# Scores on two row tiles, DMA transposes in chosen chunks, and a planner with priority tables in a fused attention and feed-forward kernel

## Chip, cores and metric

One core of a Trainium2 chip. The metric is the device time of one execution in microseconds. An execution has a state: slow ones (over 1.5% above the fastest of the same kernel) are set aside. The profiler also records the clock that was granted to TensorE; its mean is called "the clock" below (1.0 is full). A ratio of two kernels is the mean of one's fast runs over the mean of the other's fast runs in the same rounds, so it is not quite the ratio of the medians that are quoted.

## The reference

```python
# B, H, S, D = 4, 8, 768, 48;  d_model = 384, d_ff = 2048
f = 1 / (1 + exp(-f_logit))
for t in range(S):                                  # gated linear attention
    state = f[:, :, t, :, None] * state + einsum('bhd,bhe->bhde', k[:, :, t], v[:, :, t])
    y[:, :, t] = einsum('bhd,bhde->bhe', q[:, :, t], state)
x = y.transpose(0, 2, 1, 3).reshape(B * S, H * D)   # 3072 tokens x 384
h = x @ w_in
out = (h * cos(h)) @ w_out
```

## The kernel before

The sequence is cut into 24 chunks of 128 tokens. For a chunk, ScalarE turns f into running decays (an exponential, a logarithm, then two exponentials `b` and `bi` of sums that TensorE makes). q is multiplied by `b`, k by `bi`; both are transposed; TensorE makes scores, masked by VectorE, then the output y, which is transposed into x. Feed-forward units of 128 or 256 tokens follow: product with w_in, cosine on ScalarE, product on VectorE, product with w_out. Every operation is an object with candidate engines, a duration and a priority. A planner in Python, run at build time, lists them in one static order; each engine then runs its part strictly in that order.

```python
def chunk_load(b, c, prio):
    for pool, src in ((fS, f_logit), (vS, v), (kS, k), (qS, q)):
        eng, dma = {"SP": 650.0}, nc.sync
        if prio < 1 and pool in (kS, qS):            # chunk 0 only
            eng, dma = {"ACT": 600.0}, nc.scalar
        elif prio < 1 and pool is vS:
            eng, dma = {"POOL": 850.0}, nc.gpsimd
        ...

# scores: 128 rows of contraction; k of even and odd heads in two copies,
# zero where the other head's rows are
for g in range(2):
    def pe(e, g=g, pa=pa):
        for i in range(4):
            h = 4 * g + i
            nc.tensor.matmul(o[:, i, :], lhsT=kz[g].ap[:, i, :], rhs=qdt.ap[:, h // 2, :], ...)
...
# order: the earliest possible start wins, then the priority
key = (pick[1], o.prio, o.seq)
...                                                  # (cut)
pr = LEAD + RATE * n0 + 0.5 * span * j * G / KF      # first product:  2 + chunk number
pr = LEAD + LAG + RATE * n0 + 0.5 * span + 0.5 * i   # second product: 7 + chunk number
GATES = [1, 2, 3, 4]      # w_out transfers wait for k of these chunks; w_in for chunk 0
```

Of the kernel before, what the change touches and what calls it, by code (L numbers as in the profile page):

```python
# [9 lines left out]
F32 = mybir.dt.float32  # L10
# [86 lines left out]
class Plan:  # L97


    SEM = 70.0  # L100
    RING = 3500.0
# [4 lines left out]
    def op(self, eng, fn, reads=(), writes=(), prio=0.0, table=None, lat=0.0, grp=None, dma=0.0):  # L106
# [6 lines left out]
        for v in writes:  # L113
            w = getattr(v, "whole", v)
            if w.pool is not None:
                o.alloc.append(w)
            if v.writers:

                o.deps.add(v.writers[-1])
        for v in list(reads) + list(writes):  # L120
            v = getattr(v, "whole", v)
            if v.pool is not None and v not in o.vals:
                o.vals.append(v)
                v.uses += 1
# [11 lines left out]
    def run(self):  # L136
        engs = ("PE", "ACT", "DVE", "POOL", "SP")
        free = dict.fromkeys(engs, 0.0)
# [13 lines left out]
        while len(order) < n:  # L152
            best = None
            for o in ready:
                at = max([d.end + (0.0 if e0 == d.eng == "PE" else self.SEM)
                          for d in o.deps for e0 in (next(iter(o.eng)),)], default=0.0)
                ok = True
                for v in o.alloc:
                    if v.slot is not None:
                        continue  # L160
                    b = v.pool.best()
                    if b is None:
                        ok = False
                        break
                    at = max(at, b[0] + self.SEM)
                if not ok:
                    continue
# [12 lines left out]
                key = (pick[1], o.prio, o.seq)  # L180
                if best is None or key < best[0]:
                    best = (key, pick[1], o, pick[2], pick[3])
            assert best is not None, "no op can be placed: " + str(
                [(o.seq, o.eng, o.prio, lock, o.grp, [v.pool.name for v in o.alloc]) for o in ready])
            _, s, o, e, cost = best
# [14 lines left out]
            if o.dma:  # L200
                q = int(e == "POOL")
                t = max(ring[q], s + cost)
# [3 lines left out]
                rate = (0.94 if q else 0.25) if large else 0.6  # L206
# [5 lines left out]
                ring[1 - q] += both * (1.0 - (0.25 if q else 0.94)) if large else 0.4 * both  # L212
# [23 lines left out]
def kernel(  # L236
# [21 lines left out]
    GROUPS = [1] * 4 + [2] * 10  # L258
    FAST, LAG = 24, 5.0
    GATES = [1, 2, 3, 4]  # L260
    NPE, NPX, EVERY = 8, 24, 1
    LEAD, RATE = 2.0, 1.0
    UNITS = [128] * 4 + [256] * 10
# [6 lines left out]
    make_identity(nc, ident)  # L270
    umask = cpool.tile([128, 128], BF16, name="umask")
    make_upper_triangular(nc, umask, val=1.0, diag=True)
# [25 lines left out]
    qkS = slots("qk", 3, [128, 3 * NP * C], zero=700.0)  # L298
    qktS = slots("qkt", 4, [128, 3 * NP, C])
    amS = slots("am", 4, [128, 4, C])  # L300
    szS = slots("sz", 3, [128, NP, 2 * D])
    yS = slots("y", 3, [128, d_model])
    stS = slots("st", 2, [128, NP, 2 * D], F32)
# [13 lines left out]
    P = Plan()  # L317
    for pool, cost in zeroed:
# [10 lines left out]
    def load_weights(part, i, prio):  # L329
# [8 lines left out]
        gate(o, 0 if part == 0 else GATES[i])  # L338
# [5 lines left out]
    k_done, gated = {}, {}  # L344

    def gate(o, n):

        if n in k_done:
            o.deps.add(k_done[n])
        elif n >= 0:  # L350
            gated.setdefault(n, []).append(o)

    def chunk_load(b, c, prio):
        vals = []
        for pool, src in ((fS, f_logit), (vS, v), (kS, k), (qS, q)):
            t = Val(pool)
            ap = src[b, :, c * C:(c + 1) * C, :].rearrange("h p d -> p h d")
            eng, dma = {"SP": 650.0}, nc.sync
            if prio < 1 and pool in (kS, qS):
                eng, dma = {"ACT": 600.0}, nc.scalar  # L360
            elif prio < 1 and pool is vS:
                eng, dma = {"POOL": 850.0}, nc.gpsimd
            P.op(eng, lambda e, t=t, ap=ap, dma=dma: dma.dma_start(out=t.ap, in_=ap),  # L363
                 writes=[t], prio=prio, lat=2000.0, dma=980.0)
# [3 lines left out]
    def decay_group(chunks, g, prio):  # L368

        outs = []  # L370
        for (b, c, ld) in chunks:
# [8 lines left out]

            e1 = P.op({"ACT": 515.0}, act1, reads=[f], writes=[f], prio=prio, table="E", grp=g)
            P.op({"ACT": 515.0}, act2, reads=[f], writes=[sp], prio=prio, table="E", grp=g)
# [4 lines left out]
        for (b, c, ld, sp) in outs:  # L387
# [15 lines left out]
            P.op({"ACT": 400.0}, ex, reads=[pc], writes=[bt], prio=prio, table="E", grp=g)  # L403
            P.op({"ACT": 400.0}, lambda e, pc=pc, bi=bi, ex=ex: ex(e, pc, bi, 1.0, H * D),
# [4 lines left out]
    def attend(b, c, ld, bt, bi, prio):  # L409
        _, v32, kf, qf = ld  # L410
# [3 lines left out]
        qtd = qk.part(lambda a: a[:, 0:NP * C].rearrange("p (h d) -> p h d", d=64)[:, :, 0:D])  # L414
        ktd = [qk.part(lambda a, par=par: a[:, NP * C:].rearrange(
            "p (n r d) -> p n r d", r=4, d=64)[:, :, 3 * par, 0:D]) for par in range(2)]
        fast = tok < FAST * C
        E = lambda e: nc.vector if e == "DVE" else nc.gpsimd
        P.op({"POOL": 1000.0, "DVE": 560.0} if fast else {"POOL": 1000.0}, lambda e: E(e).tensor_mul(  # L419
            out=qtd.ap, in0=qf.ap,  # L420
            in1=bt.ap[:, 0:H * D].rearrange("p (h d) -> p h d", d=D)),
            reads=[qf, bt], writes=[qtd], prio=prio)
        for par in range(2):
            o = P.op({"POOL": 550.0, "DVE": 350.0} if fast and tok else {"POOL": 550.0}, lambda e, par=par: E(e).tensor_mul(  # L424
                out=ktd[par].ap, in0=kf.ap[:, par:H:2, :],
                in1=bi.ap.rearrange("p (h d) -> p h d", d=D)[:, par:H:2, :]),
                reads=[kf, bi], writes=[ktd[par]], prio=prio)
        vf = Val(vbS)
        P.op({"POOL": 510.0}, lambda e: nc.gpsimd.tensor_copy(out=vf.ap, in_=v32.ap),  # L429
             reads=[v32], writes=[vf], prio=prio)  # L430
        k_done[tok // C] = o
# [6 lines left out]
        kz = [qkt.part(lambda a, g=g: a[:, (g + 1) * NP:(g + 2) * NP, :]) for g in range(2)]  # L438
        if tok < NPE * C or tok // C % EVERY:
            for g in range(3):  # L440
                pqk = Val(miS)

                def tr(e, g=g, pqk=pqk):
                    o = pqk.ap.bitcast(BF16).rearrange("p (a n) -> p a n", n=C)
                    for i in range(NP):
# [3 lines left out]
                P.op({"PE": 4 * N128}, tr, reads=[qtd] if g == 0 else ktd, writes=[pqk],  # L449
                     prio=prio, lat=170.0)  # L450

                def evac(e, g=g, pqk=pqk):
                    o = pqk.ap.bitcast(BF16).rearrange("p (a n) -> p a n", n=C)
                    d, s = qkt.ap[:, g * NP:(g + 1) * NP, :], o[:, 0:NP, :]
                    if e == "ACT":
                        nc.scalar.copy(out=d, in_=s)
                    else:
                        nc.vector.tensor_copy(out=d, in_=s)
                P.op({"DVE": 425.0, "ACT": 500.0}, evac, reads=[pqk],
                     writes=[qdt if g == 0 else kz[g - 1]], prio=prio)  # L460
        else:
            P.op({"SP": 1400.0}, lambda e: nc.sync.dma_start_transpose(out=qkt.ap, in_=qk.ap),  # L462
                 reads=[qtd] + ktd, writes=[qdt] + kz, prio=prio, lat=2000.0, dma=2100.0)

        ams = []
        for g in range(2):
            pa, am = Val(paS), Val(amS)

            def pe(e, g=g, pa=pa):
                o = pa.ap.rearrange("p (a n) -> p a n", n=C)  # L470
                for i in range(4):
                    h = 4 * g + i
                    nc.tensor.matmul(o[:, i, :], lhsT=kz[g].ap[:, i, :],  # L473
                                     rhs=qdt.ap[:, h // 2, :], start=(i == 0), stop=(i == 3))
            P.op({"PE": 4 * N128}, pe, reads=[kz[g], qdt], writes=[pa], prio=prio, lat=170.0)

            def mask(e, pa=pa, am=am):
# [3 lines left out]
            P.op({"DVE": 670.0}, mask, reads=[pa], writes=[am], prio=prio)  # L481
            ams.append(am)
# [3 lines left out]
        if c < NCH - 1:  # L486
            ps, S_out = Val(miS), Val(szS)

            def pes(e):
                o = ps.ap[:, 0:H * D].rearrange("p (h d) -> p h d", d=D)  # L490
                for h in range(H):
                    nc.tensor.matmul(o[:, h, :], lhsT=qk.ap[:, (NP + h) * C:(NP + h + 1) * C],
                                     rhs=vf.ap[:, h, :],
                                     start=(h == 0), stop=(h == H - 1))
            P.op({"PE": 8 * 25.0}, pes, reads=ktd + [vf], writes=[ps], prio=prio, lat=170.0)
            psv = lambda: ps.ap[:, 0:H * D].rearrange("p (a n) -> p a n", n=2 * D)
            if S_in is None:
                src, srcap, cost = ps, psv, {"DVE": 550.0}
            else:
                st = Val(stS)  # L500
                P.op({"DVE": 530.0}, lambda e: nc.vector.tensor_add(  # L501
                    out=st.ap, in0=psv(), in1=S_in.ap),
                    reads=[ps, S_in], writes=[st], prio=prio)
                src, srcap, cost = st, (lambda: st.ap), {"POOL": 1000.0}
            P.op(cost, lambda e: E(e).tensor_mul(  # L505
                out=S_out.ap, in0=srcap(),
                in1=bt.ap[:, H * D:, None].broadcast_to([128, NP, 2 * D])),
                reads=[src, bt], writes=[S_out], prio=prio)
# [5 lines left out]
        def pey(e):  # L514
            o = py.ap[:, 0:H * D].rearrange("p (h d) -> p h d", d=D)
            for h in range(H):
                nc.tensor.matmul(o[:, h, :], lhsT=ams[h // 4].ap[:, h % 4, :], rhs=vf.ap[:, h, :],  # L517
# [11 lines left out]
        P.op({"ACT": 380.0, "DVE": 530.0}, copy(lambda: yt.ap, lambda: py.ap[:, 0:H * D]),  # L529
             reads=[py], writes=[yt], prio=prio)  # L530
        x = xT[tok // C]
        if tok < NPX * C:
# [8 lines left out]
            P.op({"ACT": 380.0, "DVE": 330.0}, copy(lambda: x.ap, pxv), reads=[px], writes=[x],  # L541
# [6 lines left out]
    def moe(t0, T):  # L548
# [6 lines left out]
        for j in range(KF // G):  # L555
# [10 lines left out]
            pr = LEAD + RATE * n0 + 0.5 * span * j * G / KF  # L566
# [91 lines left out]
```

## Time and profile before

| | before |
|---|---|
| median of 3 runs | 200.21 us (199.2 to 202.75, the last one slow) |
| profiled execution, its span | 198.71 us, 196.9 us |
| busy: TensorE, ScalarE, VectorE, GpSimd | 88%, 74%, 72%, 30% |

The span goes from the first to the last instruction of the trace; runs are some 2 us longer. The lines of the profile are in the prediction. "PE" is TensorE, "DVE" VectorE, "ACT" ScalarE, "POOL" GpSimd, "SP" SyncE, which issues most loads. A "q" behind an engine's name marks its instruction queue, for instance the time that issuing a load takes it. Busy time of TensorE contains the depth of its pipeline (a 384-column product is recorded as 326 ns, while in a burst one starts every 162.5), so this document counts **full-rate work**: how many matmuls started in a stretch, times the time one takes in a long burst. Stretch minus work is **lost time**.

### The profile page before, as it was taken

What the parts mean: (1) busy time and instruction counts of PE and PEld (TensorE: products, weight loads), DVE (VectorE), ACT (ScalarE), POOL (GpSimd) and SP (SyncE); (2) the same over time, 40 slices, a digit from 0 to 9 for tenths busy, and PEclk for the clock granted to TensorE, in tenths of its full rate; (3) what the DMA queues carried; (4) which work ended last, traced back from release to release, by engine and by line L of the source; (5) the groups of instructions that cost most, each with busy time, mean ns of one, the idle gap of its engine ahead of it and who ended that gap; (6) DMA issues with size and microseconds to landing.
All of it is one profiled execution on the core that took longest, in us unless ns stands there. A gap on an engine that the chain in (4) does not pass through costs nothing.

```text
span 196.9 us, 5063 instructions
## 1 busy us (share of the span) xinstructions
PE 173.7 (88%) x1968; PEld 135.7 (69%) x1968; DVE 141.3 (72%) x256; ACT 146.0 (74%) x263; POOL 58.2 (30%) x94
## 2 busy tenths in 40 slices
PE   0388987696899978999999999999999999999993
PEld 0167884485687766887876886877777788868661
DVE  5178865867897937956967978869999998928200
ACT  4457688597987975968968988989999996729210
POOL 7395104162412734205114214122332601000000
PEclk9999999999999999999999999999999999999999
DMA  7999998999899999999999999999999341020122
GB/s 139 217 179 194 188 196 173 184 202 183 163 217 190 222 171 248 234 191 223 165 226 192 212 229 192 226 221 194 221 206 260 91 97 45 0 80 3 40 80 82
DMA packets 131144, 33.36 MB, mean 169 GB/s; under 512 B 124416, under 2 KB 131072, under 8 KB 131120
## 3 DMA queue, kind: packets, MB, share of 16 engines
q1 hardware_dynamic: 125264, 29.30, 73.8%
q0 software_dynamic: 3776, 3.34, 10.7%
q10 hardware_dynamic: 2080, 0.39, 1.1%
q8 instruction: 15, 0.25, 0.5%
q14 instruction: 9, 0.07, 0.1%
HBM read 25.17 MB, written 4.72 MB: 152 GB/s over the span
## 4 chain that ended last, share of the span: by engine, by line
PE 42%; DMA 24%; DVE 11%; SPq 7%; POOL 5%; ACT 4%; issue 4%; DVEq 0%; POOLq 0%; ACTq 0%
PE ps L583 18%; PE ps L562 17%; DMA w_out_bf<-in_moe_w_out_dram 10%; DMA qkt<-qk 6%; SPq L363 5%; DMA q<-in_q_dram 4%; DMA v<-in_v_dram 4%; DVE gT L573 3%; PE ps L473 3%; DVE am L478 2%; DVE qk L419 2%; SPq L462 2%; POOL w_in_bf L336 2%; PE ps L517 1%; DVE y L527 1%
## 5 line engine op out<-in xcount | busy, mean ns | idle before, releaser
L583 PE MATMUL ps<-w_out_bf,gT 128*128 128x384 bf16 x384 | 71.2, 326 | 2.4 <-DMA w_out_bf<-in_moe_w_out_dram 2.2
L562 PE MATMUL ps<-xT,w_in_bf 128*128 128x256 bf16 (+1 forms) x672 | 69.3, 257 | 1.5 <-DVE xT L527 0.8
L562 PEld LDWEIGHTS <-w_in_bf 128*128 128x128 bf16 x672 | 57.3, 98 | 8.8 <-DVE xT L527 0.9
L573 DVE TENSOR_TENSOR gT<-ps,cosh 128x512 bf16<-128x512 f32 x96 | 60.1, 681 | 3.6 <-ACT cosh L569 3.5
L569 ACT ACTIVATE cosh<-ps 128x512 bf16<-128x512 f32 x96 | 53.7, 604 | 8.7 <-PE ps L562 6.0
L583 PEld LDWEIGHTS <-gT 128*128 128x128 bf16 x384 | 35.2, 97 | 21.1 <-issue 2.2
L478 DVE TENSOR_TENSOR am<-ps,umask 128x512 bf16<-128x512 f32 x48 | 31.0, 682 | 13.0 <-PE ps L473 12.9
L429 POOL CAST vb<-v 128x384 bf16<-128x384 f32 x24 | 12.7, 531 | 43.2 <-DMA v<-in_v_dram 28.2
L424 POOL TENSOR_TENSOR qk<-k,bi 128x192 bf16<-128x192 f32 x30 | 19.2, 650 | 20.0 <-ACT bi L401 10.2
L505 POOL TENSOR_TENSOR sz<-st,b 128x384 bf16<-128x384 f32 x16 | 13.6, 848 | 38.1 <-DVE st L501 29.1
L419 DVE TENSOR_TENSOR qk<-q,b 128x384 bf16<-128x384 f32 x20 | 13.4, 668 | 12.7 <-DMA q<-in_q_dram 7.5
L473 PE MATMUL ps<-qkt 128*128 128x128 bf16 x192 | 16.5, 225 | 2.5 <-DMA qkt<-qk 2.5
L592 ACT COPY ot<-ps 128x384 f32<-128x384 f32 x14 | 6.7, 478 | 15.2 <-PE ps L583 15.2
L625 ACT ACT_TABLE_LOAD x12 | 15.4, 1283 | 2.2 <-issue 2.0
L401 ACT ACTIVATE b<-ps 128x388 f32<-128x388 f32 x24 | 12.1, 503 | 6.2 <-PE ps L394 6.0
L569 ACT ACT_TABLE_LOAD x12 | 15.4, 1283 | 0.2
L376 ACT ACTIVATE f<-f 128x384 f32<-128x384 f32 x24 | 11.7, 518 | 4.4 <-DMA f<-in_f_logit_dram 4.3
L473 PEld LDWEIGHTS <-qkt 128*128 128x128 bf16 x192 | 12.3, 100 | 3.8 <-DMA qkt<-qk 2.8
L447 PE MATMUL ps<-ident,qk 128*128 128x128 bf16 x96 | 9.3, 242 | 5.2 <-DVE qk L419 3.2
L391 PE MATMUL ps<-sp,umask 128*128 128x384 bf16 x24 | 8.1, 346 | 5.6 <-ACT sp L379 5.2
L527 ACT CAST y<-ps 128x384 bf16<-128x384 f32 x16 | 7.7, 480 | 6.7 <-PE ps L520 3.8
L401 ACT ACTIVATE bi<-ps 128x384 f32<-128x384 f32 x24 | 12.0, 500 | 0.0
(37 smaller groups left out, 156.2 us busy)
## 6 DMA issues: line engine op xcount, KB each, us to landing
f<-in_f_logit_dram SPq DMA_DIRECT2D x24, 192.0 KB, 4.1
out_dram<-ot SPq DMA_DIRECT2D x24, 192.0 KB, 2.7
v<-in_v_dram SPq DMA_DIRECT2D x23, 192.0 KB, 4.0
k<-in_k_dram SPq DMA_DIRECT2D x23, 192.0 KB, 3.8
q<-in_q_dram SPq DMA_DIRECT2D x23, 192.0 KB, 4.3
w_in_bf<-in_moe_w_in_dram POOLq DMA_DIRECT2D x4, 384.0 KB, 9.7
w_out_bf<-in_moe_w_out_dram POOLq DMA_DIRECT2D x4, 384.0 KB, 8.3
qkt<-qk SPq DMA_TRANSPOSE x16, 4.0
```

Source lines behind the costliest of these rows:

```text
L401: nc.scalar.activation(out=o.ap, in_=pc.ap[:, 0:n], func=AF.Exp, scale=s)
L419: P.op({"POOL": 1000.0, "DVE": 560.0} if fast else {"POOL": 1000.0}, lambda e: E(e).tensor_mul(out=qtd.ap, in0=qf.ap, in1=bt.ap[:, 0:H * D ...
L424: o = P.op({"POOL": 550.0, "DVE": 350.0} if fast and tok else {"POOL": 550.0}, lambda e, par=par: E(e).tensor_mul(out=ktd[par].ap, in0=kf. ...
L429: P.op({"POOL": 510.0}, lambda e: nc.gpsimd.tensor_copy(out=vf.ap, in_=v32.ap), reads=[v32], writes=[vf], prio=prio)
L473: nc.tensor.matmul(o[:, i, :], lhsT=kz[g].ap[:, i, :], rhs=qdt.ap[:, h // 2, :], start=(i == 0), stop=(i == 3))
L478: nc.vector.tensor_mul(out=am.ap, in0=pa.ap.rearrange("p (a n) -> p a n", n=C), in1=umask[:, None, :].broadcast_to([128, 4, C]))
L505: P.op(cost, lambda e: E(e).tensor_mul(out=S_out.ap, in0=srcap(), in1=bt.ap[:, H * D:, None].broadcast_to([128, NP, 2 * D])), reads=[src, ...
L562: nc.tensor.matmul(ph.ap[:, g * T:(g + 1) * T], lhsT=w_in_bf[:, m, f0:f0 + 128], rhs=x[:, m, :], start=(g == 0 and m == 0), stop=(g == G - ...
L569: P.op({"ACT": 570.0}, lambda e, ph=ph, co=co: nc.scalar.activation(out=co.ap, in_=ph.ap, func=AF.Sin, bias=HALF_PI), reads=[ph], writes=[ ...
L573: P.op({"DVE": 650.0}, lambda e, ph=ph, co=co, gv=gv: nc.vector.tensor_mul(out=gv.ap, in0=ph.ap.rearrange("p (g t) -> p g t", t=T), in1=co ...
L583: nc.tensor.matmul(po.ap[:, 0:d_model], lhsT=gT.ap[:, j, i * 128:(i + 1) * 128], rhs=w_out_bf[:, j, :], start=(j == 0), stop=(j == KF - 1))
L625: nc.scalar.preload_act_table_set("natural_log_exp_and_others")
```

## The change

The intent: cheaper scores, less work for the DMA engines, and an order in which TensorE waits less. The planner's durations are also brought nearer to a trace. The diff, cut to its core:

```diff
-    GROUPS = [1] * 4 + [2] * 10
-    FAST, LAG = 24, 5.0
-    GATES = [1, 2, 3, 4]
-    NPE, NPX, EVERY = 8, 24, 1
-    LEAD, RATE = 2.0, 1.0
-    UNITS = [128] * 4 + [256] * 10
+    GROUPS = [1, 1, 1, 1, 1, 1, 2, 2, 2, 2, 1, 1, 3, 2, 3]
+    UNITS = [128, 128, 128, 128, 256, 256, 256, 256, 128, 128, 256, 256, 256, 256, 128, 128]
+    ATT = [-10.16, -8.17, ...]       # 24 numbers each: attention, decay groups,
+    DEC = [-0.66, -1.41, ...]        # first product, second product
+    MM1 = [6.38, -2.33, ...]
+    MM2 = [8.02, 8.08, ...]
+    GATES = [1, 0, 0, 0, 2, 3, 2, 2]
+    QUEUES = ["SAAA", "ASSA", "SSSS", ...]           # f, k, q, v: S SyncE, A ScalarE
+    QK_DMA = [7, 10, 13, 14, 15, 17, 18, 19, 20, 21, 22, 23]
+    X_DMA = [11, 13, 15, 18, 19, 20, 22, 23]
+    FAST = 12
@@ the planner's choice
-                key = (pick[1], o.prio, o.seq)
+            # per engine: best priority among those that can start within WAIT of the first
+            for p in sorted(picks, key=lambda p: p[:2]):
+                if p[4] not in best and p[2] <= first[p[4]] + self.WAIT.get(p[4], 0.0):
+                    best[p[4]] = p
@@ loads
-            if prio < 1 and pool in (kS, qS): ... nc.scalar
-            elif prio < 1 and pool is vS: ... nc.gpsimd
+            way = QUEUES[min(b * NCH + c, len(QUEUES) - 1)][len(vals)]
@@ scores (q and k each in one block of four, two heads of 48 rows per 128)
+        def pe(e):
+            for p in range(NP):
+                for g in range(2):
+                    nc.tensor.matmul(pas[g].ap[:, p * C:(p + 1) * C],
+                                     lhsT=kdt.ap[64 * g:64 * g + D, p, :],
+                                     rhs=qdt.ap[64 * g:64 * g + D, p, :], ...)
```

(Cut: the state update in four products of two heads with its additions split by rows, the transposes, new durations.)

## The prediction

> **What bounds the kernel now.** I read four views, in this order: the page's head (busy time, slices, queues), the groups of instructions, the same busy times cut into three stages, and the chain of waits. First the head:
>
> ```profile
> span 196.9 us, 5063 instructions
> PE 173.7 (88%) x1968; PEld 135.7 (69%) x1968; DVE 141.3 (72%) x256; ACT 146.0 (74%) x263; POOL 58.2 (30%) x94
> PE   0388987696899978999999999999999999999993
> DMA  7999998999899999999999999999999341020122
> q1 hardware_dynamic: 125264, 29.30, 73.8%
> q0 software_dynamic: 3776, 3.34, 10.7%
> q10 hardware_dynamic: 2080, 0.39, 1.1%
> ```
>
> Two resources are full. TensorE is ragged over the first third and full after it; the DMA engines are full until slice 31 (155 us) and then nearly idle. VectorE and ScalarE stay near three quarters. The stages say where TensorE loses:
>
> ```profile
> core 0: us, PE busy (x) PEld busy (x) DVE busy (x) ACT busy (x) POOL busy (x), PEclk, DMA share, GB/s
> 0.00:50.00 50.00, 34.66 (x485) 28.32 (x486) 33.54 (x67) 33.03 (x57) 21.40 (x39) 1.00 1.10 186
> 50.00:155.00 105.00, 101.00 (x1151) 79.16 (x1150) 85.55 (x155) 90.78 (x168) 34.65 (x53) 1.00 1.02 206
> 155.00:197.00 42.00, 38.04 (x337) 28.18 (x334) 22.24 (x37) 22.19 (x41) 2.16 (x3) 1.00 0.19 58
> ```
>
> Busy time counts the pipeline's depth with every short burst, so I work with full-rate time instead, read off long bursts in the chain of waits:
>
> ```profile
> 27.51 2.68 PE ps L562 x48
> 38.25 1.46 PE ps L583 x8
> 74.61 0.62 PE ps L473 x8
> 109.95 0.65 PE ps L583 x4
> 110.60 3.93 PE ps L562 x36
> 114.53 0.45 PE ps L473 x8
> 116.93 0.20 PE ps L517 x8
> 117.13 0.17 PE ps L520 x4
> ```
>
> So one matmul takes, at full rate, 3.93/36 = 109 ns at 256 columns, about 57 ns at 128 columns (2.68/48 and 0.45/8), 0.65/4 = 162.5 ns at 384, 25 ns at 48 and 43 ns at 96. With the counts of the groups: second product 384 x 162.5 = 62.4; first product 480 x 109 + 192 x 57 = 63.3; scores 192 x 56 = 10.8; q/k transposes 96 x 56 = 5.4; scores times v 192 x 25 = 4.8; state update 160 x 25 = 4.0; state read 80 x 43 = 3.4; x transposes 72 x 56 = 4.0; decay sums 6.3. Sum **164.5 us** of work in a span of 196.9, so TensorE loses 32.4. Doing the same sum with the counts of the first 50 us gives about 29 of work: 21 are lost there. The last matmul ends at 193.6: 3.3 for the last copy and store. The remaining 8 are spread over 50 to 193 us. The lost time of the first 50 us is fill (the first chunk's chain) and weights that come late:
>
> ```profile
> 13.09 13.55 DMA w_out_bf<-in_moe_w_out_dram
> 31.95 6.25 DMA w_out_bf<-in_moe_w_out_dram
> ```
>
> **DMA is a second bound of almost the same size.** Queue q10 carried two input loads in 1.1% of 196.9 = 2.17 us, so 1.08 us of all 16 engines each. A store costs about 0.54 (share 0.19 over the last 7 us, some two and a half stores). q1 took 145.3 us: 93 loads 100.4, 24 stores 13.0, which leaves 31.9 for 16 transposes, 2.0 each. A late chunk costs the DMA 4 x 1.08 + 2.0 + 0.54 = 6.9 us, and TensorE 164.5/24 = 6.85. The loads feed it just fast enough, never ahead.
>
> **What the Trainium skill says.** TensorEngine Tiling (Array Packing), sections Theoretical Speedup and Key Properties: a contraction of at most 64 rows may run up to twice as fast as two row tiles working in parallel, and changing the tiling mode drains TensorE. The trace of before has only 128*128 forms, so it shows neither. TensorE: Matmul & The Clock Gate, section Back-to-back issue gap: columns/2.4 + 2.5 ns, 56 at 128 columns; bursts here agree (56), not with its 81 for sustained pairs. ScalarE: Activation LUTs, section What ACT_TABLE_LOAD costs: 1283 ns plus a drain of about 1380. The trace has 24 loads of 1283, while idle time before the twelve at L569 sums to 0.2 us, so I count no drain. DMA: Bandwidth & Descriptors, section Specifications: line rate needs 512 B or more. The loads have rows of 48 floats, 192 B; 1.08 us for 196,608 B is 182 GB/s, and the change leaves those rows alone.
>
> **The change part by part.** Counts come from the changed kernel's built instruction order.
> - Scores: still 192 matmuls, now 48 rows of contraction on two 64-row tiles, alternating between tiles and two banks. Fully parallel they cost 5.4 us, not parallel 10.8. The new planner figure is 330 ns a chunk, 7.9 us; I take that: **-2.9**, before any drain.
> - x transposes on TensorE: 72 become 48: -1.3. State update: 160 x 25 becomes 80 x 43: -0.6. Four more units of 128 tokens: 96 x 109 becomes 192 x 57: +0.4. q/k transposes stay 96: chunks come in two groups rather than three, but 12 chunks instead of 8. TensorE: 164.5 - 4.4 = **160.1**.
> - DMA: 12 transposes of two thirds the size, 12 x 1.33 = 16.0, plus 8 of x at a quarter, 8 x 0.5 = 4.0, in place of 31.9: **-12**. The DMA per chunk falls to about 5.7 on average, 1 us below TensorE's 6.7, so that loads can run ahead; most transposes sit in chunks 13 and later.
> - ScalarE: table loads 24 to 18, -7.7; xT copies 12 to 5, y copies 16 to 19, q/k copies 5 to 3: some -3.5. Busy 146 to about 135. VectorE: q and k products fall from 20 + 18 halves (23.2 us) to 19 whole (about 12); the split state additions (64 rows, 192 elements) add 2 to 3: 141 to about 132. GpSimd takes 29 whole products of about 1.0 us in place of 4 + 30 halves (23.2): about 68. All three have room; this mainly shortens waits of TensorE, so I do not add it.
> - Weights: all eight transfers were gated after k of chunks 0 to 4 (GpSimd issues 9.5 to 42.1 us). Now w_in follows v of chunks 0 and 1, and w_out v of chunks 2 and 3. The first chunk itself gains little: ScalarE issues five loads before its first table load, the fifth waiting for an earlier one to land, which may delay its first exponential from 4.1 to about 6; in return k no longer queues on GpSimd.
> - Order: tables of priorities and a planner with other durations decide which chunk and unit goes first. This removes no work; it decides how much of the 32 lost microseconds stays.
>
> Sum. Lost in the first 50 us: 21 less 4.5, since the 3.5 us weight waits beside w_out and the holes that followed between 30 and 50 (some 6 lost there) should mostly close: 16.5. Lost from 50 to the last matmul: 8 less 3, as the loads run ahead: 5. Tail 3.3. So 160.1 + 24.8 = a span of 184.9. The runs exceed the span: the profiled execution by 1.8 us (198.71 against 196.9), the lowest run by 2.3. I add 1.6, leaning to the fast side since the tables look searched for: **186.5 us**.
>
> **The rivals.**
> 1. Drain takes the tiling's gain. Each chunk switches mode in and out, 48 switches; an isolated 128-column matmul lasts 219 ns against 56 at full rate, so a full drain may be some 160 ns (an estimate from these). That is up to 7.7 us, more than the 2.9 saved; then 190 to 192. For it: short runs of scores between other work. Against: the planner's 330 ns looks like a measurement, and two drains might overlap with weight loads.
> 2. DMA still sets the pace early. Weights (21 us of q0) and the first six chunks (26 us) fill the DMA for 47 us whatever the order; earlier weights push chunk loads back, and TensorE loses again what it gained. Then the 21 stays near 20 and the time is 190. The full DMA row of slices 1 to 9 speaks for it; against it, TensorE needs only two or three chunks once the weights are in.
> 3. The order works much better than I allow: lost time in the first 50 us down to 13, in the middle to 2, and full parallel scores: a span near 176, 178 us. For it: 24-entry tables come from a search. Against: a planner's static order is only as good as its durations, and in-order queues stop at each wrong guess.
> 4. GpSimd's longer chain (q and k product, 2 us, then cast, from chunk 12 on) starves a late chunk. At about 3.6 us a chunk against 6.7 it can only hurt in latency.
>
> **Range and chances.** Centre 186.5; rivals 1 and 2 bring it to 190 to 192, both together to 195; rival 3 to 178. Range 180 to 192. Two per cent faster means under 196.2, which needs only a third of the sum: faster 0.95, within 2% 0.04, slower 0.01.
>
> **What would show it.** Right: score groups in a 64*128 form with about 41 ns between starts; full-rate work of TensorE near 160; hardware queue q1 about 12 us shorter; 18 table loads; DMA row falling off before 150 us; the first w_out waits gone and 5 us less lost in the first 50 us. Wrong: gaps of over 100 ns around each score group (rival 1); loads or v casts still waited for between 20 and 50 us (rival 2); ScalarE or VectorE over 85% busy in the middle, which would make one of them the bound; or a new long hole where one engine waits in order for a late piece.

## The result

The changed kernel is correct. Its median is **194.13 us** (193.2 to 194.2, 4 runs) against 199.81 for the kernel before (now 4 runs); the ratio is 0.971 (95% interval 0.967 to 0.975). The direction was right; the time lies outside the predicted range of 180 to 192, and the gain is 6 us in place of 14.

The head of the page of the changed kernel (busy times, the 40 slices, the queues):

```profile
span 192.4 us, 5056 instructions
PE 170.5 (89%) x1960; PEld 129.5 (67%) x1960; DVE 138.0 (72%) x259; ACT 137.4 (71%) x250; POOL 65.6 (34%) x105
PE   0056996879999999999999999999999999999992
PEclk9999997899999999999999999999999999999999
DMA  6999999998995999996399899799993383102022
q1 hardware_dynamic: 114096, 26.55, 68.9%
q10 hardware_dynamic: 5200, 0.98, 3.1%
```

Against the kernel before, TensorE starts later (the first slices read 0 0 5 6 in place of 0 3 8 8) and is at 9 from slice 10 on, without the dips that the kernel before has until slice 16. The row PEclk, all 9 before, has a 7 and an 8 in slices 7 and 8. The first two of the three stages that the prediction shows for the kernel before:

```profile
core 0: us, PE busy (x) PEld busy (x) DVE busy (x) ACT busy (x) POOL busy (x), PEclk, DMA share, GB/s
0.00:50.00 50.00, 32.70 (x416) 26.03 (x417) 33.15 (x66) 31.15 (x51) 17.95 (x35) 0.97 1.11 187
50.00:155.00 105.00, 104.00 (x1201) 78.69 (x1200) 83.98 (x159) 87.93 (x165) 42.77 (x64) 1.00 0.90 183
```

In the first 50 us only 416 matmuls began; before it was 485. In full-rate work, lost us of each stretch (each matmul counted once, in the stretch in which it starts; a tiled score counted at 41 ns):

| kernel | 0 to 25 | 25 to 50 | 50 to 150 | after the last matmul |
|---|---|---|---|---|
| before | 14.3 | 7.7 | 5.9 | 3.4 |
| changed | 17.9 | 6.7 | 3.6 | 3.6 |
| changed, two loads later (below) | 15.9 | 5.1 | 3.5 | 3.6 |
| changed, f first (below) | 14.6 | 5.9 | 3.5 | 3.6 |

So the middle is better than it was, and the start worse. TensorE's waits in the first 50 us say the same: it waits 9.4 us for its first input in place of 5.2, and no longer for weights, where before it waited 2.6. Why it is worse stands in the timeline of ScalarE and its queue; first the kernel before, then the changed kernel (columns: start, us, engine, line, what; in brackets the idle time ahead and what ended it):

```profile
0.73 0.48 ACTq L363 DMA_DIRECT2D k<-in_k_dram  x1
1.24 0.74 ACTq L363 DMA_DIRECT2D q<-in_q_dram  x1
2.02 1.28 ACT L625 ACT_TABLE_LOAD   x1 [2.02 <-issue]
4.12 0.52 ACT L376 ACTIVATE f<-f 128x384 f32<-128x384 f32 x1 [0.82 <-DMA f<-in_f_logit_dram]
```

```profile
0.74 0.48 ACTq L388 DMA_DIRECT2D k<-in_k_dram  x1
1.25 0.74 ACTq L388 DMA_DIRECT2D q<-in_q_dram  x1
2.02 1.19 ACTq L388 DMA_DIRECT2D v<-in_v_dram  x1
3.24 1.65 ACTq L388 DMA_DIRECT2D f<-in_f_logit_dram  x1
4.93 2.00 ACTq L388 DMA_DIRECT2D v<-in_v_dram  x1
6.96 1.28 ACT L648 ACT_TABLE_LOAD   x1 [6.96 <-issue]
8.25 0.52 ACT L401 ACTIVATE f<-f 128x384 f32<-128x384 f32 x1
```

The five issues take 6.06 us of ScalarE's queue, because each takes longer than the one before (0.48 up to 2.00 us). SyncE issues loads in the same time; that this is what slows them is not tested. The table load and the first exponential, on which chunk 0 hangs, come 4.1 us later. The planner holds an issue for 0.6 us.

The second thing to see is in the scores. TensorE's timeline around one group in the changed kernel:

```profile
106.94 5.40 PE L585 MATMUL ps<-xT,w_in_bf 128*128 128x256 bf16 x48
112.27 0.40 PE L489 MATMUL ps<-qkt 48*128 48x128 bf16 x8
112.60 0.82 PE L606 MATMUL ps<-w_out_bf,gT 128*128 128x384 bf16 x4
```

Single starts from the same trace, in us:

```
112.066  last 256-column product
112.271  112.274    112.337  112.340    112.392  112.396    112.448  112.452   eight scores
112.600  next product
```

Eight scores start as four pairs, about 56 ns apart: the two row tiles do run side by side. But the first pair comes 205 ns behind a product that takes 109, and the next product 148 ns behind the last pair, where 56 would do. Over all 24 groups the medians are 258 ns ahead (a 384-column product, 162 of it its own), 182 inside, 148 behind. So the way in costs 258 - 162 = 96 ns, and the way out 148 - 56 = 92. A group costs 96 + 182 + 148 = 426 ns. On 128 rows, in the kernel before, it is 391 + 56 = 447.

### The profile page after: what moved, and what is told of

It is laid out like the page before. It is cut to its first block, busy times and chain, and to the rows that moved or that the text cites. A ratio compares the mean times of both kernels' runs of the same rounds, so it can differ in the third digit from the quotient of the medians.

```text
span 192.4 us, 5056 instructions
## 1 busy us (share of the span) xinstructions
PE 170.5 (89%) x1960; PEld 129.5 (67%) x1960; DVE 138.0 (72%) x259; ACT 137.4 (71%) x250; POOL 65.6 (34%) x105
## 4 chain that ended last, share of the span: by engine, by line
PE 78%; DVE 8%; ACT 3%; issue 3%; ACTq 3%; DMA 2%; DVEq 0%
PE ps L585 33%; PE ps L606 29%; PE ps L489 4%; PE ps L470 3%; ACTq L388 3%; DVE qk L447 3%; PE ps L540 2%; DVE am L496 2%; PE ps L416 2%; PE ps L508 2%; DMA out_dram<-ot 2%; PE ps L561 1%; PE ps L543 1%; DVE st L523 1%; ACT L648 1%
## 5 line engine op out<-in xcount | busy, mean ns | idle before, releaser
L585 PE MATMUL ps<-xT,w_in_bf 128*128 128x128 bf16 (+1 forms) x768 | 69.5, 251 | 0.6 <-DVE xT L550 0.4
L585 PEld LDWEIGHTS <-w_in_bf 128*128 128x128 bf16 x768 | 60.9, 100 | 6.6 <-issue 0.9
L527 POOL TENSOR_TENSOR sz<-st,b 64x192 bf16<-64x192 f32 x32 | 16.1, 503 | 52.0 <-DVE st L523 39.0
L447 POOL TENSOR_TENSOR qk<-k,bi 128x384 bf16<-128x384 f32 x16 | 16.0, 1003 | 7.5 <-ACT bi L426 7.3
L447 POOL TENSOR_TENSOR qk<-q,b 128x384 bf16<-128x384 f32 x13 | 13.0, 1001 | 12.0 <-ACT b L426 8.7
L648 ACT ACT_TABLE_LOAD x9 | 11.5, 1283 | 7.1 <-issue 7.0
L523 DVE TENSOR_TENSOR st<-ps,sz 64x192 f32<-64x192 f32 x32 | 11.3, 352 | 4.1 <-PE ps L508 3.2
L476 DVE COPY qkt<-ps 128x512 bf16<-128x512 bf16 x21 | 8.4, 420 | 7.7 <-PE ps L470 7.6
L447 DVE TENSOR_TENSOR qk<-q,b 128x384 bf16<-128x384 f32 x11 | 8.1, 740 | 7.1 <-ACT b L426 7.0
L404 ACT ACTIVATE sp<-f 128x384 bf16<-128x384 f32 x24 | 12.6, 523 | 0.7
L419 PEld LDWEIGHTS <-sp 128*128 128x128 bf16 x96 | 6.2, 100 | 10.1 <-issue 8.1
```

The costliest lines, as they stand in the source:

```text
L404: nc.scalar.activation(out=sp.ap[:, :, 0:D], in_=f.ap, func=AF.Ln, bias=1.0)
L447: lambda e, src=src, w=w, dst=dst: E(e).tensor_mul(out=dst.ap, in0=src.ap, in1=w.ap[:, 0:H * D].rearrange("p (h d) -> p h d", d=D)),
L523: P.op({"DVE": 370.0}, lambda e, g=g, sg=sg: nc.vector.tensor_add(out=sg.ap, in0=psv(g), in1=block(S_in.ap, g)), reads=[ps, S_in], writes= ...
L527: o = P.op(cost, lambda e, g=g, srcap=srcap, out=out: E(e).tensor_mul(out=out.ap, in0=srcap(), in1=bt.ap[rows(g), H * D:, None].broadcast_ ...
L585: nc.tensor.matmul(ph.ap[:, g * T:(g + 1) * T], lhsT=w_in_bf[:, m, f0:f0 + 128], rhs=x[:, m, :], start=(g == 0 and m == 0), stop=(g == G - ...
L648: nc.scalar.preload_act_table_set("natural_log_exp_and_others")
```

## The experiments

The kernel before took between 198.6 and 207.9 us in the four batches, at clocks of 0.959 to 1.0. So the kernels are compared with each other at equal clock, and their ratio to before is quoted only with its interval.

**Theory A**: the start is late because ScalarE issues five loads ahead of its first table load. **Theory B**: the DMA sets the start, whichever queue issues.

### 1. Queues of the first loads as before

```diff
-    QUEUES = ["SAAA", "ASSA", "SSSS", ...]
+    QUEUES = ["SAAP", "SSSS"]
```

> The changed kernel, with only the queues of the first chunks' loads put back as in the kernel before: f of chunk 0 and all of chunk 1 from SyncE, k and q of chunk 0 from ScalarE, v of chunk 0 from GpSimd. The planner lays the rest out anew. Theory A (ScalarE issues five loads for 6.2 us before it can load its table, so the first exponential starts at 8.25 us instead of 4.12 and everything behind it, to the end, is late): first exponential back near 4.1 us, first product L585 starts 3 to 5 us earlier than 19.6, time 190 to 191 against 194.1. Theory B (the start is bound by the DMA, which must bring weights and chunks in any order): first exponential early, but the first 50 us still lose 23 to 24 us of TensorE and the time stays within 1 us of 194.

Measured: 192.78 us (192.22 to 193.14), clocks 0.982 to 0.989, ratio to before 0.961 (0.951 to 0.972). The first exponential is back at 4.26 us, but the planner, told of other queues, made another order for the whole kernel, and TensorE ran at half clock from 27.9 to 34.7 us. Faster than the changed kernel by 1.4 (by 1.5 to 2.1 at clocks near 0.99) and not by 3 to 4: it supports A's first step, and is confounded in its size.

### 2. The same five issues in the kernel before

```diff
-            if prio < 1 and pool in (kS, qS): ... nc.scalar
-            elif prio < 1 and pool is vS: ... nc.gpsimd
+            if (prio < 1 and pool is not fS) or (prio == 1 and pool in (fS, vS)):
+                eng, dma = {"ACT": 600.0}, nc.scalar
```

> The kernel before, with one part of the change alone: k, q and v of chunk 0 and f and v of chunk 1 issued from ScalarE. Theory A: its first exponential moves from 4.1 to about 8 us and the time rises by 2 to 4 us, to 202 to 204. Theory B: the w_out waits between 26 and 38 us absorb it, the time stays within 1 us of 200.

Measured: 200.79 us (199.89 to 201.78), ratio 1.001 (0.990 to 1.013). The first exponential did move, to 8.32 us, but at clocks of 0.997 to 1.0 the kernel took 199.9 to 201.0, where the kernel before takes 199.3 and 200.0 at 1.0 in another batch: about 1 us, short of the 2 to 4 that A put. Theory B's answer, within 1 us, is met as well as any. It seems that the kernel before hides most of the delay behind other waits, and that a late first chain costs what the order behind it cannot absorb; that was not followed up here. It has to be tested in the changed kernel itself.

### 3. Two of the five loads later, the plan untouched

The planner's order is kept for every engine; only two instructions move within ScalarE's, behind its first two activations (an exponential and the logarithm). The later experiments start from this kernel or from that of section 8, but for one run of section 4 and that of section 10.

```diff
     order = P.run()
+    loads = [o for o in order if o.dma and o.eng == "ACT"]
+    first = [o for o in order if o.table is not None][:2]
+    late = loads[3:5]                              # f and v of chunk 1
+    order = [o for o in order if o not in late]
+    at = order.index(first[1]) + 1                 # behind the first two activations
+    order[at:at] = late
```

> The changed kernel with exactly the same plan on every engine, but the last two of the five loads that ScalarE issues (f and v of chunk 1) moved behind its first two exponentials. Theory A: the first exponential starts at about 4.6 us (three issues, then the table load) instead of 8.25, chunk 0 is done some 3 us earlier, and the time falls by 1 to 3 us; f and v of chunk 1 land later, which can give some of it back. Theory B: no change within 1 us.

Measured: 190.52 us (190.29 to 191.32), clocks 1.0, 1.0, 0.998, 0.991. From ScalarE's timeline of this run:

```profile
3.34 1.28 ACT L654 ACT_TABLE_LOAD   x1 [3.34 <-issue]
4.63 0.52 ACT L401 ACTIVATE f<-f 128x384 f32<-128x384 f32 x1
```

To put a size on it, the changed kernel and this one ran again on one chip:

> The changed kernel again, as a control on the same chip as the next three. Expected 193 to 194.5, with one half-clock window of 3.4 us near 30 us in most executions, as in its first trace (granted clock 0.99).

> The kernel with the two loads of chunk 1 behind the first two exponentials, again, beside the changed kernel on the same chip. Theory A (the five issues on ScalarE delay the start): 3 to 4 us faster than the changed kernel, most of it from the first chain, about 1 from the half-clock window that is then missing. If the first result was luck of the clock: less than 2 us faster.

| | clock 0.998 to 1.0 | clock 0.989 to 0.991 |
|---|---|---|
| changed | 192.74, 193.14 | 194.27, 194.29 |
| two loads later | 190.23, 190.34 | 191.27, 191.34 |

At equal clock the two loads are worth 2.5 to 3 us; the medians differ by 2.9, a little under the 3 to 4 expected. Theory A is shown, for this kernel: same instructions, same order elsewhere. The table shows something more: each of these two kernels has two times, 0.9 to 1.6 us apart, by its clock.

### 4. The scores without row tiles

The scores use all 128 rows, so two heads are summed: wrong, same count and order.

```diff
-                                     lhsT=kdt.ap[64 * g:64 * g + D, p, :],
-                                     rhs=qdt.ap[64 * g:64 * g + D, p, :],
+                                     lhsT=kdt.ap[:, p, :],
+                                     rhs=qdt.ap[:, p, :],
```

> The changed kernel with the score products on all 128 rows, same instructions and order, so the scores are wrong on purpose (two heads summed). In the trace of the changed kernel eight scores start in four pairs 56 ns apart, but each group has about 92 ns of gap ahead of it and behind it. If the switch of tile form costs those gaps, a group costs 0.41 us tiled and 0.45 not, and this kernel is slower by 24 x 0.04 = 1 us (0.5%). If the tiling saves what the prediction put in, 2.9 us, it is slower by that, 1.5%. If tiles cost more than they give, it is faster.

> The same with scores on all 128 rows (wrong on purpose). In the traces a tiled group takes 96 ns ahead + 182 + 148 ns = 0.426 us and one on 128 rows 391 + 56 = 0.447 us, so tiling saves 24 x 0.021 = 0.5 us: slower by 0.3 to 0.8 us than the control. The prediction's figure would be 2.9 us.

Measured: in the changed kernel 193.87 us (193.37 to 194.93); in the one with two loads later 191.97 (190.84 to 192.19). At equal clock the second pair, from one chip, gives 190.84 against 190.34 (0.997 and 0.998) and 191.82 to 192.19 against 191.27 to 191.34 (near 0.99): 0.5 to 0.9 us slower. The trace of the second, around the same place:

```profile
104.48 5.40 PE L585 MATMUL ps<-xT,w_in_bf 128*128 128x256 bf16 x48
109.72 0.61 PE L489 MATMUL ps<-qkt 128*128 128x128 bf16 x8
110.16 0.81 PE L606 MATMUL ps<-w_out_bf,gT 128*128 128x384 bf16 x4
```

The gaps are gone: 109.72 is 109 ns behind the last start of L585, and 110.16 less 109.72 is 0.44. The working from the trace, 24 x (447 - 426) = 0.5 us, fits; the 2.9 us of the prediction does not.

### 5. More work for the DMA, nothing else

In the kernel with two loads later, the q/k transposes carry a third, unused block, as large as those of the kernel before.

```diff
-    qkS = slots("qk", 4, [128, 2 * NP * C], zero=470.0)
-    qktS = slots("qkt", 4, [128, 2 * NP, C])
+    qkS = slots("qk", 4, [128, 3 * NP * C], zero=470.0)
+    qktS = slots("qkt", 4, [128, 3 * NP, C])
```

> The same plan, but the twelve q/k transposes by DMA carry a third, unused block again as in the kernel before (393 KB each instead of 262): about 0.66 us more of the DMA each, 8 us in all, and nothing else. If the middle of the kernel got quicker because the DMA has less to do, 50 to 155 us lose 2 to 3 us more and the time rises by as much. If the new order alone filled the middle, it stays within 1 us of the control.

Measured: 191.78 us (190.31 to 192.38), against 190.81 for the control on the same chip. In the traces, TensorE is busy for 104.01 us of the stage from 50 to 155 us, against 104.00 in the control, and by full-rate work it loses 3.5 us from 50 to 150 in both: its middle did not change. But the profiled execution is the fastest of the four. The others took 191.33 at clock 1.0, 192.38 at 0.999 and 192.22 at 0.991, where the control took 190.23 and 190.34, and 191.27 and 191.34. So up to 2 us stays possible in single executions, 0.8 in the mean.

The bytes rose by 1.57 MB as meant. The time of queue q1 rose by 74.4% of 188.5 less 72.8% of 188.6 = 2.9 us; but the same kernel, in its first trace, has 133.0 us in place of 137.3, so the figure is uncertain by more than it says, and the 8 us expected are neither shown nor excluded. DMA relief was not seen to fill the middle, as far as this part of it goes; that it gives up to 1 us is not excluded.

### 6. The tables made flat

In the kernel with two loads later; the planner lays everything out anew.

```diff
-    ATT = [-10.16, ...]; DEC = [-0.66, ...]; MM1 = [6.38, ...]; MM2 = [8.02, ...]
+    ATT = [0.0] * 24;    DEC = [0.0] * 24;   MM1 = [2.0] * 24;  MM2 = [7.0] * 24
```

> The kernel with the two loads later, but the tables of priorities made flat: 0 for every chunk and decay group, 2 and 7 for the two products as in the kernel before. Same instructions. If the tables are what fills the middle (3 us less lost there than before, which the bigger transposes did not take away again): 2 to 5 us slower, lost after 50 us. If the new planner rule and sizes do it without the tables: within 1 us.

Measured: 202.44 us (201.2 to 203.26) at clocks of 0.973 to 0.982, ratio to before 1.014 (1.007 to 1.020): the gain of the whole change is gone. TensorE loses 14.5 us from 50 to 150 us in place of 3.5, of which 8.0 lie between 125 and 150:

```profile
PE   0359977799998799998999999849999999999992
PEclk9999999999999999999999999966999999999999
```

The hole in slices 26 and 27 is followed by a dip of the clock in 27 and 28. The new planner rule and durations without the tables do not fill the middle. Whether the tables do it, or any plan other than the one that they were fitted to loses as much, this run cannot tell; section 7 bears on that.

### 7. Weights gated otherwise, the plan made anew

```diff
-    GATES = [1, 0, 0, 0, 2, 3, 2, 2]
+    GATES = [0, 0, 0, 0, 1, 2, 3, 4]      # first run: as before
+    GATES = [-1, -1, 0, 0, 2, 3, 2, 2]    # second run: two w_in not gated at all
```

> The kernel with the two loads later (190.3 to 191.3), but the eight weight transfers gated as in the kernel before (w_in after chunk 0, w_out after chunks 1, 2, 3, 4; the gate is the cast of v). The planner lays the rest out anew. If earlier weights are worth the 4.5 us that the prediction gave them: 194 to 195, with the w_out waits of 5 us and more back between 26 and 40 us. If they only push the chunk loads back by as much as they gain: within 1 us of 190.8, the loss moved from 10 to 30 us into 30 to 50 us.

> The kernel with the two loads later, and the first two weight transfers not gated at all: they start at about 2 us beside the loads of chunk 0. The planner lays the rest out anew. If the start is a matter of what the DMA brings first (rival 2 of the prediction): the loads of chunk 0 land 2 to 4 us later, the first exponential or the first product of q moves back by as much, and the time is 1 to 4 us longer. If weights are what the first stage waits for, 1 to 2 us faster.

Measured: 203.09 us (200.04 to 205.25, two of four runs slow) and 201.0 (199.15 to 201.11). Both lie outside what either theory put, and for a reason that makes them useless for the question: the loss is spread over the whole kernel (in the first, 11.5 us lost between 50 and 125 us, where the control loses 3.1). Both keep the tables. It looks as if these were fitted to one plan, and a planner fed with another gate lays out a different one that they do not fit; so what fills the middle would be this plan and its tables together (the plan made anew in section 1 kept it: 3.6 us lost). What follows is a rule for the rest: move single instructions in the finished plan, do not plan again.

### 8. The start mended further

f of chunk 1 becomes SyncE's second load; v of chunk 1 goes behind the four activations of chunk 0 on ScalarE. (The diff is cut: f0 is SyncE's first load.)

```diff
+    first = [o for o in order if o.table is not None][:4]
+    f1, v1 = loads[3:5]
+    f1.fn.__defaults__, f1.eng = (t, ap, nc.sync), "SP"
+    order.insert(order.index(f0) + 1, f1)
+    order.insert(order.index(first[3]) + 1, v1)
```

> The kernel with the two loads later, changed once more in the start alone, the plan else the same: f of chunk 1 comes from SyncE as its second load, v of chunk 1 from ScalarE behind the four exponentials of chunk 0. ScalarE then is not held by an issue at 6.5 to 7.0 us, and its exponential for chunk 1 should start at about 8 us in place of 10.1. If the chain of the first chunks sets the start: 1 to 2 us faster than 190.8. If the weights set it (first w_in lands near 16 us): within 0.5 us.

Measured: 189.91 us (three runs of 189.69 to 189.93 at clock 1.0; one slow), ratio 0.949 (0.945 to 0.953). The exponential of chunk 1 starts at 7.04 us. That is 0.4 us faster than the kernel of section 3 at clock 1.0 (190.23 to 190.42, in other batches), where A put 1 to 2; it is the answer of the other theory, within 0.5 us if the weights set the start. It is correct and the fastest kernel, 5.1% under the kernel before.

On top of it, v of chunk 0 from GpSimd as before the change:

> The kernel with f first, and v of chunk 0 issued from GpSimd as in the kernel before, so that ScalarE issues only two loads ahead of its table load. The first exponential starts at 4.1 instead of 4.56 us. If this chain still sets the start: 0.3 to 0.6 us faster than 189.8 at full clock. If v of chunk 0, which gates the weights, lands later from that queue: the same or slower.

Measured: 190.26 us (190.07 to 190.76), first exponential at 4.19. No gain: v of chunk 0 is cast at 8.29 us from either queue, and the first w_in is issued right behind it. The first exponential, 0.37 us earlier, brought nothing: the start of chunk 0's chain no longer sets the time. Not every drop of the clock costs time, either: this kernel took 190.07 and 190.4 at 0.991 and 0.989, and 190.11 at 1.0.

### 9. The weights alone, in the finished plan

In the kernel of section 8 (the diff is cut: `w_in`, `w_out`, `k2`, `v_cast` and `user` are picked out of the order).

```diff
+    for o, after in zip(w_out[:3], (w_in[3], k2, v_cast[3])):
+        order.insert(order.index(after) + 1, o)
+    order.insert(order.index(user), w_out[3])       # just ahead of its first user
```

> The kernel with f first (189.7 to 189.9 at full clock), the same order on every other engine, but the four w_out transfers issued where the kernel before issued them: two early (near 12 and 18 us in place of 22 to 23), the third near 29, the last behind a cast near 40 us in place of 29. If earlier weights are worth what the prediction gave them, 4.5 us: 193 to 195, with TensorE waiting for the last w_out near 41 us. If the plan's weights gain little because the chunk loads wait instead: within 1.5 us of 190.

Measured: fast runs 193.08 to 193.51 at clocks of 0.982 to 0.988, two slow ones at 0.964 (197). Against 189.8 at clock 1.0, in another batch, that is 3.5 us, within the first answer. But it is no test of early against late: two w_out transfers are issued earlier than in the kernel of section 8 (at 13.0 and 16.7 us in place of 22.2 and 23.0) and two later (30.6 and 35.9 in place of 27.0 and 29.4). The trace (of a slow run) has three waits that the kernel of section 8 has not:

```profile
27.46 0.52 ACT L401 ACTIVATE f<-f 128x384 f32<-128x384 f32 x1 [1.78 <-DMA f<-in_f_logit_dram]
28.65 0.48 PE L416 MATMUL ps<-sp,umask 128*128 128x384 bf16 x1 [1.53 <-ACT sp L404]
42.05 1.44 PE L606 MATMUL ps<-w_out_bf,gT 128*128 128x384 bf16 x4 [0.91 <-DMA w_out_bf<-in_moe_w_out_dram]
```

The f of the first line was issued at 10.50 us and landed at 27.44; in the kernel of section 8 it was issued at 10.59 and landed at 23.47. So the two early w_out push a chunk's load back by 4 us, as rival 2 of the prediction says, and a late one is waited for. Around both places TensorE ran at half clock (27.5 to 34.3 and 41.1 to 47.9 us), where the kernel of section 8 has no such stretch. How much of the 3.5 us is an early w_out, a late one or the clock I cannot separate.

### 10. Is the half clock caused by idle TensorE?

The clock records of the traces have stretches at half clock, in multiples of 3.41 us. Beside them, the share of the 3.41 us ahead in which TensorE was busy:

```
kernel                    half clock      busy share just ahead
changed                   31.5 to 34.9    0.41
changed, again            31.8 to 35.2    0.40
old routes                27.9 to 34.7    0.44
later, no tiles           28.2 to 31.6    0.47
two loads later           none            lowest after the rise to full clock: 0.54
f first                   none            0.63
```

These six suggest a threshold near 0.5, but the other traces do not bear it out. Half clock also followed busy shares of 0.53 to 0.70 (tables flat 0.58; weights as before 0.60; weights not gated 0.53, 0.61 and 0.70), and did not follow 0.42 (v of chunk 0 from GpSimd), 0.48 (bigger transposes) and 0.49 (before). Full-rate work sorts them better. I cut all 17 traces into windows of 3.41 us from the rise to full clock on, and left out those behind the last matmul: all nine windows at full clock with under 0.40 of work were followed by half clock, none with over 0.48, and two of thirteen in between. This was seen afterwards and is not tested.

A test in the changed kernel, where TensorE waits for y of chunk 2:

```diff
             def tx(e):
+                for _ in range(32 if tok == 2 * C else 0):
+                    nc.tensor.matmul(px.ap[:, 0:128], lhsT=ident, rhs=ident, start=True, stop=True)
                 for t in range(KM):
```

> The changed kernel, with 32 useless 128-column products put in front of the three x transposes of chunk 2, where TensorE stands idle for some 2 us near 28 us. [...]If that idle stretch is the cause, no execution has a half-clock window near 31 us, all four show a clock of 0.998 to 1.0 and 192.7 to 193.3 us, though there is more work. If the clock drops for another reason, half of the executions stay at 0.99 and 194.2.

TensorE's timeline there, in the changed kernel and then with the filler (the second view ends at 33.0 us, inside the last burst):

```profile
30.26 0.34 PE L561 MATMUL ps<-ident,y 128*128 128x128 bf16 x3 [1.82 <-DVE y L550]
31.05 3.61 PE L585 MATMUL ps<-xT,w_in_bf 128*128 128x128 bf16 x36 [0.21 <-DVE xT L550]
```

```profile
29.21 1.95 PE L561 MATMUL ps<-ident 128*128 128x128 bf16 x32
31.20 0.34 PE L564 MATMUL ps<-ident,y 128*128 128x128 bf16 x3
31.99 1.22 PE L588 MATMUL ps<-xT,w_in_bf 128*128 128x128 bf16 x19 [0.21 <-DVE xT L550]
```

In the changed kernel 36 products take 3.61 us, 100 ns each, most of them at half clock; at full rate they take 57. With the filler 19 take 1.22, and all 36 take 2.17 us. No execution had a clock under 0.999: 192.62 us (192.55, 192.57, 192.67 at 1.0 and 193.45 at 0.999). Without the filler, five of the changed kernel's eight executions were at 0.989 to 0.991 and took 194.1 to 194.3, three at 0.998 to 1.0. Useless work made the kernel about 1.6 us faster than the five, and cost nothing against the three. So the idle stretch is the cause of this half-clock window. It does not bring one every time: three of the eight executions did without, and f first has the same wait of 1.82 us (at 26.96) and kept the full clock.

## Why the prediction was wrong, point by point

The prediction's span was 184.9 us; the trace has 192.4. The 7.5 between them:

- **"The first chunk itself gains little", and lost time of the first 50 us "21 less 4.5 ... 16.5": this step failed.** Measured are 24.6, about 0.5 of it the ways into score tiles; the kernel before, counted in the same way, lost 22.0. Three things made it fail:
  - The prediction saw the five issues and let them cost "from 4.1 to about 6"; it was 8.25 (its figure fits issues of 0.6 us, as the planner has them), and it put no cost on the delay. In the changed kernel it costs 2.5 to 3 us (shown).
  - The idle stretch behind it brings the half clock, 1.1 to 1.6 us (shown), a cost that the prediction did not have at all.
  - The 4.5 for weights did not come. TensorE's waits for weights did go, as it said; but in the kernel before they sum to 2.6 us, and with the start mended the first 50 us still lose 20.5. This is where rival 2 put it: near 20 lost and a time of 190, measured 189.9. In the kernel of section 8 one can see a load pushed back: a k issued at 23.92, beside w_out transfers issued at 22.2 to 29.4, takes 12.9 us to land; VectorE waits 2.2 us for it, and then TensorE 1.7. Loads were pushed back in the kernel before too (a k issued at 14.94 took 16 us), so it seems that the shift of transfers moved this loss rather than ended it. How many of the some 3.4 us that are left are due to it was not tested apart, since moving the gates in the planner changed everything else, and moving the transfers alone (section 9) mixed early and late ones; that stays open.
- **Scores, "I take that: -2.9, before any drain": mis-sized.** Two tiles run in parallel, as the page on tiling said they may; the switch takes 96 ns in and 92 out, as rival 1 warned, where the prediction feared that "a full drain may be some 160 ns", and 0.5 us is left. The planner's 330 ns is exactly what lies from the first score to the next product (182 + 148): it contains the way out and not the way in. So 24 x 96 ns = 2.3 us of the 7.5 are here (shown).
- **Middle, "8 less 3, as the loads run ahead: 5": the right size, and a cause that was not confirmed.** From 50 us to the last matmul 3.9 us are lost, in place of 6.9 before, and 1.8 of the 3.9 are the ways into score tiles, which the prediction left out of its sum. Bigger transposes did not visibly take the gain back; a plan with flat tables did (14.5 lost from 50 to 150 us), and so did two of the three plans made anew with the tables (section 7). The prediction said of the order that it "removes no work; it decides how much of the 32 lost microseconds stays", and then gave it no number.
- DMA, "-12": q1 and q10 together went from 74.9% of 196.9 = 147.5 us to 72.0% of 192.4 = 138.5 in one trace of the changed kernel and 73.5% of 192.5 = 141.5 in the other, so by -6 to -9. The 2.0 us of a transpose was worked out as a remainder; section 5 could not measure it.
- VectorE, 141 "to about 132": measured 138.
- Right: the counts, 18 table loads of 1283 ns, ScalarE and GpSimd (137 and 66 us busy against about 135 and 68), the tail of 3.3 (3.6), and that no other engine becomes a bound.

Sum, in round numbers: scores +2.3; first 50 us +7.6 without the score tiles (of it issues about 2.8, clock about 1.4, the rest 3.4 open as said); middle -2.9 without the score tiles; tail +0.3. That is 7.3 of 7.5. The middle's better figure hides part of the miss at the start: the near hit, 194 against a range that ends at 192, is partly luck.

## What to carry to other kernels

Before trusting a gain in the steady part, walk through the first chain instruction by instruction, and look whether an engine that computes issues loads ahead of its first work: here such an issue took 0.48 to 2.00 us, not the planner's 0.6. Whether that costs anything is a matter of the order behind it: 2.5 to 3 us in the changed kernel, about 1 or nothing in the kernel before. Count a switch of tile form on its way in as well as on its way out, and let groups be long. Where an order comes from tables fitted to one plan, change single instructions in the finished plan: every new plan made here but one (section 1) lost the whole gain.

## What the Trainium skill lacked or had wrong

- TensorEngine Tiling (Array Packing), section Key Properties: says that a change of tiling mode drains TensorE, without a size. Here: 96 ns on the way in and 92 on the way out between 128 rows and two tiles of 64; inside, the two scores of a pair start 3 to 4 ns apart and the pairs about 56, so "up to 2x" is reached while it lasts. Eight 128-column matmuls gain only 21 ns of 447.
- TensorE: Matmul & The Clock Gate, section What's actually happening: half rate comes after at least one idle window of about 3.4 us. The stretches here are multiples of 3.41 us, which agrees; but no idle window was needed: a gap of 1.8 us was enough in five of eight executions, with TensorE busy for 0.40 of the window ahead, and in other traces for up to 0.70. In full-rate work the windows ahead of a half-clock stretch had 0.11 to 0.48 (17 traces). Its rule of no idle gaps over some 3 us (Why this matters for your kernels) is too mild for this kernel.
- ScalarE: Activation LUTs, section What ACT_TABLE_LOAD costs: adds a drain of about 1380 ns to each switch of table set. The 1283 ns are in the traces of both kernels, the drain is not: the exponential behind the first load starts 8.25 - 6.96 - 1.28 = 0.01 us after it, and each of the 17 later loads of the changed kernel starts 17 to 19 ns behind the operation before it.
- DMA: Bandwidth & Descriptors gives a first-byte latency, but I found no figure for how long the issuing engine is held when loads queue up. Here the same issue on ScalarE took 0.48 us first and 2.00 us as the fifth, and one of SyncE 6.81 us while w_in moved.
- No page that I read says that a half-clock window in the middle of a kernel comes in some executions and not in others, so that their times fall into groups: 192.7 to 193.2 and 194.1 to 194.3 us for the changed kernel, 190.2 to 190.6 and 191.3 with two loads later.
